# A gated mix of a long convolution and local attention: x transposed on the way in, and three groups of loads put elsewhere in their queue

## The chip, the cores and the metric

The kernel runs on one core of a Trainium2 chip. The core has a matrix engine (TensorE, PE in the profile; its weight loads are PEld), a vector engine (VectorE, DVE), a scalar engine (ScalarE, ACT), GpSimd (POOL) and a small engine that here only issues transfers (SyncE, SP). Sixteen DMA engines move data for all of them. Each engine runs its own instructions in order and waits on semaphores for the others. The metric is the device time of one execution in microseconds; the number of record is the median over the runs.

## The reference

S is 2048 positions, D is 640 channels, everything is bfloat16. Two branches are computed and mixed by a gate:

```python
x = A_q
g = sigmoid((x * gate_w).sum(-1, keepdims=True))
return g * a + (1 - g) * b

# a: shift convolution (4 taps) of k, times v, then a long causal convolution by FFT, times q
kv = k_shift * v
y  = irfft(rfft(kv padded to 2S) * rfft(ssm_k padded to 2S))[:S] + kv * ssm_D
a  = q * y

# b: attention of 32 heads of 20 channels; each position looks at 8 earlier
#    positions, two apart, itself included
q, k, v = split(x @ wqkv)
b = softmax(q k^T / sqrt(20)) v  @ wo
```

## The kernel before, in words

**A planner writes the order.** The kernel describes its work as generators (`loads`, `transposes`, `vproj`, `qkproj`, `fragger`, ...). Each yields requests: an engine, a cost in ns, the events it depends on, PSUM slots. A small list scheduler (`Plan`) picks at each step the request with the earliest start plus 120 ns times a priority from the table `PR`, and the instructions are emitted in that order. So the order on every engine, and on the SP queue, is settled when the kernel is built; an event in the plan that has no data behind it moves an instruction in the order but adds no wait on the chip. DMA issues on SP go round eight completion semaphores, so an issue waits until the eighth issue before it has landed.

**Attention first.** x is loaded in four chunks into `xS` with positions on partitions (even positions, then odd ones, since attention looks back in steps of two). TensorE transposes it in 128x128 blocks (L520), and the blocks are copied from PSUM into `xT` (channels on partitions, L277 and L279), which has gaps of seven zero columns ahead of each half. From `xT` come the values (`psv`, L540, in two halves of the channels) and the queries and keys (`pj`, L602). Queries and keys are copied out to `Gs` and `sH`, and POOL moves each head's 20 rows ("fragments", L638) to three rotating sets `qb` and `kb`. For eight groups of four heads: scores (`sc`, L668), exponential on ScalarE (L676), values (`O`, L702), and division on VectorE (L714, L716) into `oS`.

**Convolution beside it.** VectorE computes the four taps and the product with v in four blocks (L480 to L497); the product is written to DRAM (`kv_scr`) and read back in another layout. The filter `ssm_k` comes in two halves (`load_h`) over the place of the used k blocks; POOL adds `ssm_D` to its first sample (L802). The long convolution is a two-stage transform of 4096 points: stage 1 (L738) with `F1b`, stage 2 (L760) with the 2 MB matrix `G`, which takes the place of the staging `Gs`, first for the filter (`Hs`), then for kv (`X`). Complex products need a copy of the filter's spectrum with its two partition halves exchanged ("turned"): `swaps` makes it by DMA, group by group of channels, L835, and for the last group in two halves, L844, the second of which must wait for the multiplies of the first pass. `mults` (L858, L862) multiplies in two passes, groups 0 to 2 and groups 3 and 4, four blocks each. `inverse1` (L875) needs the blocks of its pass, `inverse2` (L950) needs all of `inverse1`, the matrix `T` (loaded over the last turned group once pass two is done) and q, which is loaded again as `qg` and scaled by the gate (L927).

**End.** Attention's output is transposed (L894), multiplied by `wo` (L988), scaled by 1 - g on the way out of PSUM (L995), moved to q's layout by POOL's DMAs (L1004), added (L1012) and stored (L975).

The order of the SP queue around the change, by its emission before:

```
x0 (two parts), Wv0, x1, x2, x3, Wqk ...
... kv stores 3 2, filter half 0, kv stores 1 0, G, filter half 1, kv back, wo
... swaps of groups 0 to 3, first half of group 4, 12 loads of q,
    second half of group 4, 4 loads of q, T, stores of the output
```

Of the kernel before, what the change touches and what calls it, by code (L numbers as in the profile page):

```python
# [144 lines left out]

PR = {'warm': -10.0, 'loads': 0.0, 'o_slot': -41.5, 'fragger': -30.7, 'score_gen': -0.4, 'pv_gen': -0.8, 'masks': 1.1, 'wcopy': 3.5, 'halo_gen': -13.7, 'conv': 17.2, 'transposes': 1.3, 'vproj': 2.4, 'gate': 2.4, 'qkproj': 3.1, 'h_diag': 16.3, 'h_stream': 1.9, 'open_p3': 26.5, 'swaps': -47.2, 'u_stream': 7.3, 'mults': -6.7, 'inverse1': 11.0, 'otrans': 10.8, 'outproj': 6.2, 'load_t': 18.2, 'load_q': 8.6, 'qscale': 0.8, 'adds': -3.0, 'inverse2': 25.0, 'vproj1': 4.5, 'vevict': -4.9, 'qevict': -6.0, 'opearly': 14.6, 'oplate': 22.1, 'vlean': 5.0, 'qlean': -169.0, 'slean': 204.0, 'ilean': 93.0, 'olean': 20.0, 'uh': 17.9}
HEAD = dict(A=130.0, D=60.0)
# [102 lines left out]
def kernel(  # L250
# [38 lines left out]
    ident = p0.tile([128, 128], BF, name="ident")  # L289
    xS = p0.tile([128, 16, D], BF, name="xS", tag="oS")  # L290
    Wv = p0.tile([128, NDT, D], BF, name="Wv", tag="wo")
# [39 lines left out]
    pL = Lx.enter_context(tc.tile_pool(name="pL", bufs=1, side="left", reuse_waits="tile"))  # L331
    xT = pL.tile([128, NDT, XW], BF, name="xT")
    Wqk = pL.tile([128, NDT, 2, D], BF, name="Wqk")
    pa = pL.tile([128, 4, D], BF, name="pa")
    pb = pL.tile([128, 4, D], BF, name="pb")
    wl = pL.tile([128, 4, D], BF, name="wl")

    W3 = B_wqkv.rearrange("(t p) (w n) -> p t w n", p=128, w=3)
# [3 lines left out]
    def ev(name):  # L342
        if name not in E:
            E[name] = Ev()
        return E[name]
# [10 lines left out]
    def loads():  # L356
# [4 lines left out]

        def load_x(c, k0=0, k1=4):
            yield from load(f"x{c}{k0}", xS[:, 4 * c + k0:4 * c + k1, :], xq4[:, c // 2, 4 * (c % 2) + k0:4 * (c % 2) + k1, :],
                            163840 * (k1 - k0), 1280)

        def nat(src, a):
            return raw(src, 4 * a * D, [[16 * D, 128], [1, 4 * D]])

        yield from load("ident", ident[:], ca["ident"].ap(), 32768, 256)
        yield from load_x(0, 0, 2)  # L370
        yield from load_x(0, 2, 4)
        yield from load("Wv0", Wv[:, :, 0:320], W3[:, :, 2, 0:320], 409600, 640)
        yield from load_x(1)
        yield from load_x(2)
        yield from load_x(3)
        def load_w(w, part, c0, c1):
# [59 lines left out]
    def pool_head():  # L436
        for c0, c1 in ((0, PRE), (HS, HS + PRE), (2 * HS, XW)):
# [12 lines left out]
        plan.at["G"] = 24000.0  # L450
# [61 lines left out]
    def transposes():  # L512
        for c in range(4):
            for k0, k1, d0, nd in ((0, 2, 0, 5), (2, 4, 0, 5)) if c == 0 else ((0, 4, 0, 4), (0, 4, 4, 1)):
                nk = k1 - k0
                g = yield Req("P", 56.0 * nk * nd, [ev(f"x{c}{k0}"), ev("ident")], take=1, ins=nk * nd)
                tr = psum(g, "trx", (128, 16 // nk, 128 * nk), BF)
                for dd in range(nd):
                    for k in range(nk):
                        nc.tensor.transpose(tr[:, dd, 128 * k:128 * k + 128], xS[:, 4 * c + k0 + k, 128 * (d0 + dd):128 * (d0 + dd) + 128], ident[:, :])  # L520
                w = 128 * nk * nd
                r = yield Req("AD", dict(A=190.0 + 0.834 * w, D=150.0 + 0.54 * w), [g.done], give=g.banks)
                o = ccol(4 * c) + 128 * k0
                copy(r.eng, xT[:, d0:d0 + nd, o:o + 128 * nk], tr[:, 0:nd, :])
                mark(f"xT{c}{k0 + d0}", r)
        mark("xS", r)

    def xdeps(c):
        return [ev(f"xT{c}{d}") for d in (0, 4 if c else 2)]

    def vproj():
        for half in range(2):
            c0 = 320 * half
            for b0 in range(0, NB, 2):
                nb = min(2, NB - b0)
                g = yield Req("P", 5 * nb * 136.0, xdeps(min(3, (b0 + nb - 1) // 4)) + [ev(f"Wv{half}")], take=1, pri=PR["vproj"] if half == 0 else PR["vproj1"], ins=5 * nb)
                ps = psum(g, "psv")
# [78 lines left out]
    def fragger():  # L616
# [10 lines left out]
        for t in range(NT):  # L627
            for f, w, h in sorted(todo[t]):
# [197 lines left out]
    def swaps():  # L826

        for g in range(NG):
# [10 lines left out]
            for hf in range(2):  # L839
# [5 lines left out]
                for k in range(2):  # L845
                    mark(f"hw{g}{2 * hf + k}", r)

    def mults():
# [54 lines left out]
    def load_q():  # L903
        yield Req("G", 1.0, [ev("us1")])
# [110 lines left out]
    def o_slot():  # L1015
        yield Req("G", 1.0, [ev("xS")])
        oS = p0.tile([128, NB, D], BF, name="oS", tag="oS")
        st["oS"] = oS
        x = ev("oSfree"); x.t = 0.0
# [62 lines left out]
```

## Time and profile before

| | |
|---|---|
| median of 8 runs | 241.11 us (240.37 to 242.01) |
| the profiled execution | 241.75 us |
| its span, first to last instruction | 240.0 us |
| mean granted TensorE clock in it | 0.906 |
| DMA | 42.57 MB, mean 177 GB/s |

The profile is of one execution. Its span is shorter than its time by what lies around the first and the last instruction. A timeline line has the start and the length in us, the engine, the line of the kernel, the operation with its output and input, how many it covers, and in brackets how long the engine had been idle before it and what released it. A table by stage has, for each stretch, its length, the busy time of PE, PEld, DVE, ACT and POOL (with counts), the granted clock, the busy share of the DMA engines and GB/s. TensorE's busy time is an upper view, since matmuls overlap.

### The profile page before, as it was taken

To read this page: it belongs to the slowest core of one execution; us is meant where nothing else is said; L and a number is where in the kernel's file an instruction comes from. 1 tells how busy PE (TensorE), PEld (TensorE's weight loads), DVE (VectorE), ACT (ScalarE), POOL (GpSimd) and SP (SyncE) were. 2 spreads that over 40 slices of the span, in tenths; PEclk is the share of its full clock that TensorE was granted. 3 is DMA by queue.
4 is the path that set the end of the run, shared out by engine and by line. 5 is a ranking of instruction groups with operands and counts; after the bars stand their busy time and mean duration, and the time that the engine had idled before them with its cause. 6 is when DMAs were issued, how large, how long until landed. Compare 5 with 4: busy or idle time off the path is not lost. (4 is left out here: it accounts for less than half of the span.)

```text
span 240.0 us, 8121 instructions
## 1 busy us (share of the span) xinstructions
PE 209.3 (87%) x3526; PEld 157.6 (66%) x3526; DVE 172.5 (72%) x214; ACT 183.7 (77%) x225; POOL 68.0 (28%) x137
## 2 busy tenths in 40 slices
PE   7999999999999999888866999989799959999800
PEld 3775645555555566565645788778689949989700
DVE  0567457988797797878784999898997095069760
ACT  4438588779899898889994998899999955943520
POOL 8803721396706053150000000000303030047520
PEclk9999999999999999955555899999999997999955
DMA  6997599767779822399999509995699916015872
GB/s 185 354 331 286 104 291 307 231 165 226 190 145 175 207 53 62 115 202 206 159 175 332 196 3 201 208 201 97 141 193 196 188 43 195 11 57 162 232 216 56
DMA packets 52579, 42.57 MB, mean 177 GB/s; under 512 B 27216, under 2 KB 47824, under 8 KB 52544
## 3 DMA queue, kind: packets, MB, share of 16 engines
q1 hardware_dynamic: 47664, 32.70, 56.4%
q0 software_dynamic: 4688, 9.03, 14.5%
q8 instruction: 27, 0.44, 0.8%
q10 hardware_dynamic: 192, 0.33, 0.5%
q14 instruction: 8, 0.07, 0.1%
HBM read 23.51 MB, written 5.25 MB: 120 GB/s over the span
## 5 line engine op out<-in xcount | busy, mean ns | idle before, releaser
L676 ACT ACTIVATE ET<-sc 128x726 bf16<-128x726 f32 (+1 forms) x80 | 64.9, 863 | 5.1 <-PE sc L668 4.7
L602 PE MATMUL pj<-xT,Wqk 128*128 128x363 bf16 (+3 forms) x250 | 48.4, 343 | 0.0
L1004 POOL DMA_DIRECT2D bl<-room x32 | 16.8, 529 | 82.3 <-ACT room L995 82.3
L602 PEld LDWEIGHTS <-Wqk 128*128 128x128 bf16 x250 | 22.9, 97 | 18.4
L279 DVE CAST Hs<-s 128x1024 bf16<-128x1024 f32 (+1 forms) x26 | 28.6, 1145 | 4.3 <-PE s L738 4.2
L277 ACT CAST X<-s 128x1024 bf16<-128x1024 f32 (+1 forms) x32 | 28.0, 987 | 0.2
L540 PE MATMUL psv<-Wv,xT 128*128 128x320 bf16 x170 | 24.9, 299 | 0.4 <-DMA Wv<-in_B_wqkv_dram 0.4
L875 PE MATMUL i<-M,Hs 128*128 128x128 bf16 x160 | 21.9, 235 | 3.2 <-DVE Hs L858 2.9
L988 PE MATMUL op<-wo,Hb 128*128 128x320 bf16 x160 | 23.9, 301 | 0.4 <-ACT X L277 0.2
L277 ACT CAST X<-i 128x1024 bf16<-128x1024 f32 x20 | 19.8, 1072 | 5.4 <-PE i L875 5.4
L875 PEld LDWEIGHTS <-Hs 128*128 128x128 bf16 x160 | 20.9, 151 | 3.3 <-DVE Hs L858 3.2
L875 PE MATMUL i<-M,X 128*128 128x128 bf16 x160 | 21.8, 234 | 0.5 <-DVE X L862 0.5
L760 PEld LDWEIGHTS <-Gs 64*128 64x128 bf16 x512 | 18.6, 95 | 5.4 <-issue 4.9
L988 PEld LDWEIGHTS <-Hb 128*128 128x128 bf16 x160 | 21.3, 145 | 1.1 <-issue 0.2
L668 PE MATMUL sc<-qb,kb 31*128 31x121 bf16 x544 | 18.8, 243 | 3.4 <-DVE oS L716 1.1
L875 PEld LDWEIGHTS <-X 128*128 128x128 bf16 x160 | 20.8, 151 | 0.8 <-DVE X L862 0.8
L995 ACT ACTIVATE room<-op,omg 128x640 bf16<-128x640 f32 x16 | 13.1, 820 | 10.3 <-PE op L988 10.3
L540 PEld LDWEIGHTS <-xT 128*128 128x128 bf16 x170 | 16.1, 98 | 6.9 <-issue 0.5
L638 POOL DMA_DIRECT2D qb<-Gs x21 | 11.5, 552 | 32.2 <-ACT Gs L277 20.5
L668 PEld LDWEIGHTS <-kb 31*128 31x128 bf16 x544 | 10.4, 102 | 14.3 <-issue 11.7
L277 ACT CAST Hs<-s 128x1024 bf16<-128x1024 f32 (+1 forms) x18 | 15.4, 909 | 3.6 <-PE s L738 2.2
L702 PEld LDWEIGHTS <-ET 128*128 128x128 bf16 x544 | 15.9, 100 | 3.4 <-issue 1.9
(77 smaller groups left out, 351.3 us busy)
## 6 DMA issues: line engine op xcount, KB each, us to landing
X<-Hs SPq DMA_DIRECT2D x16, 256.0 KB, 6.6
Hb<-in_A_k_dram SPq DMA_DIRECT2D x4, 640.0 KB, 10.3
kv<-in_A_v_dram SPq DMA_DIRECT2D x4, 640.0 KB, 12.7
kv_scr<-Hb SPq DMA_DIRECT2D x8, 320.0 KB, 4.2
Hb<-in_A_ssm_k_dram SPq DMA_DIRECT2D x16, 160.0 KB, 4.5
kv<-kv_scr SPq DMA_DIRECT2D x8, 320.0 KB, 5.4
bl<-room POOLq DMA_DIRECT2D x32, 80.0 KB, 3.2
qg<-in_A_q_dram SPq DMA_DIRECT2D x16, 160.0 KB, 7.2
```

Of the source, the lines that this page charges most:

```text
L277: nc.scalar.copy(dst, src)
L279: nc.vector.tensor_copy(dst, src)
L540: nc.tensor.matmul(ps[:, bb, 0:320], lhsT=xT[:, dt, BP * (b0 + bb):BP * (b0 + bb) + 128], rhs=Wv[:, dt, c0:c0 + 320], start=(dt == 0), sto ...
L602: nc.tensor.matmul(ps[:, i, 0:n], lhsT=Wqk[:, dt, w, 128 * ft:128 * ft + 128], rhs=rhs, start=(dt == 0), stop=(dt == NDT - 1))
L668: nc.tensor.matmul(scs[h4 // 2][:, h4 % 2, BP * bb:BP * bb + BP], lhsT=kb[r:r + DH + NF, 128 * b:128 * b + 128], rhs=qb[r:r + DH + NF, BP ...
L676: nc.scalar.activation(ETs[e][:, :, 0:nw], scs[hf][:, :, 0:nw], ACT.Exp, scale=SCALE)
L702: nc.tensor.matmul(O[:, o0:o0 + 21], lhsT=ET[:, hh, BP * bb:BP * bb + 128], rhs=VW[:, b, 4 * t + h4, :], start=True, stop=True, skip_group ...
L760: nc.tensor.matmul(ps[:, c, 0:64 * n * m].rearrange("p (a j l) -> p a j l", j=m, l=16)[:, :, jj, :], lhsT=G[rows, j, rr, :], rhs=raw(a, 20 ...
L875: nc.tensor.matmul(o, lhsT=piece(A[:, g:g + 1, :])[:, 0, c, :, :, 8 * oc + il].rearrange("p q j -> p (q j)"), rhs=M[:, k, :], start=(k == ...
L988: nc.tensor.matmul(op[:, k, 0:320], lhsT=raw(a, HS * (t % 2) + t // 2, [a.ap[0], [8, 128]]), rhs=wo[:, ft, 320 * k:320 * k + 320], start=( ...
L995: nc.scalar.activation(blt, op[:, :, 0:320], ACT.Copy, scale=omg[:, gcol(t):gcol(t) + 1])
L1004: nc.gpsimd.dma_start(bl[32 * gg:32 * gg + 32, t - 1:t + 1, :].rearrange("p t c -> p (t c)"), raw(row, 0, [[4 * pitch, 32], [1, 1280]]))
```

## The change

x is loaded straight into `xT` by five transposing DMAs of 256 to 512 positions (the first one ahead of `Wv0`), and the tile `xS` goes away. The odd half [...] first 9 and last 7 positions are loaded plainly into a corner of `wl`, transposed by five small TensorE transposes and copied in. The filter's second half is loaded ahead of `G` and planned behind POOL's last fragment; q's loads are planned behind the last swap. `xT` is wider (2080 columns instead of 2072, used through a shifted view). The priorities `PR` are those of a new search, so the order on all engines changes in places.

```diff
@@ tiles
-    xS = p0.tile([128, 16, D], BF, name="xS", tag="oS")
...
-    xT = pL.tile([128, NDT, XW], BF, name="xT")
+    xTt = pL.tile([128, NDT, 2080], BF, name="xT")
+    xT = xTt[:, :, 9:2080]
...
+    xs = wl[0:16, 0, :]
@@ loads
-        def load_x(c, k0=0, k1=4):
-            yield from load(f"x{c}{k0}", xS[:, 4 * c + k0:4 * c + k1, :], xq4[:, c // 2, 4 * (c % 2) + k0:4 * (c % 2) + k1, :],
-                            163840 * (k1 - k0), 1280)
+        def load_x(name, par, n0, n):
+
+            o = 16 + n0 if par == 0 else 9 + HS + PRE + n0
+            g = yield Req("S", 600.0, move=n * 5.4)
+            nc.sync.dma_start_transpose(xTt[:, :, o:o + n], raw(x2, (2 * n0 + par) * D, [[2 * D, n], [1, D]]))
+            mark(name, g)
...
+        yield from load_x("x0a", 0, 0, 256)
+        yield from load("Wv0", Wv[:, :, 0:320], W3[:, :, 2, 0:320], 409600, 640)
+        yield from load_x("x0", 0, 256, 256)
         yield from load("ident", ident[:], ca["ident"].ap(), 32768, 256)
-        yield from load_x(0, 0, 2)
-        yield from load_x(0, 2, 4)
-        yield from load("Wv0", Wv[:, :, 0:320], W3[:, :, 2, 0:320], 409600, 640)
-        yield from load_x(1)
-        yield from load_x(2)
-        yield from load_x(3)
+        yield from load("xs0", xs[0:9], raw(x2, D, [[2 * D, 9], [1, D]]), 11520, 1280)
+        yield from load("xs1", xs[9:16], raw(x2, (2 * 1017 + 1) * D, [[2 * D, 7], [1, D]]), 11520, 1280)
+        yield from load_x("x1", 0, 512, 512)
+        yield from load_x("x2", 1, 9, 512)
+        yield from load_x("x3", 1, 521, 496)
...
-            deps = [ev(f"st{a}{c}") for a in ((2, 3) if half == 0 else (0, 1)) for c in range(2)]
+            deps = [ev(f"st{a}{c}") for a in ((2, 3) if half == 0 else (0, 1)) for c in range(2)] + [ev("fraggo")] * half
...
         yield from store_kv(0)
+        yield from load_h(1)
         for jb in range(4):
             for d, h in zip(pieces(Gs[:, 2048 * jb:2048 * (jb + 1)]), pieces(cf["G"].ap()[:, 2048 * jb:2048 * (jb + 1)])):
                 yield from load(f"G{jb}", d, h, 262144, 1024, [ev("stg21"), ev("stg30"), ev("stg31")])
-            ev(f"G{jb}").t += 2000.0
-        yield from load_h(1)
@@ transposes
-        for c in range(4):
-            for k0, k1, d0, nd in ((0, 2, 0, 5), (2, 4, 0, 5)) if c == 0 else ((0, 4, 0, 4), (0, 4, 4, 1)):
...
-                        nc.tensor.transpose(tr[:, dd, 128 * k:128 * k + 128], xS[:, 4 * c + k0 + k, 128 * (d0 + dd):128 * (d0 + dd) + 128], ident[:, :])
...
+        g = yield Req("P", 250.0, [ev("xs1"), ev("ident")], take=1, ins=5)
+        tr = psum(g, "trx", (128, NDT, 16), BF)
+        for dd in range(NDT):
+            nc.tensor.transpose(tr[:, dd, :], xs[:, 128 * dd:128 * dd + 128], ident[0:16, 0:16])
+        r = yield Req("D", 200.0, [g.done])
+        nc.vector.tensor_copy(xT[:, :, HS + PRE:HS + PRE + 9], tr[:, :, 0:9])
+        r = yield Req("D", 200.0, give=g.banks)
+        nc.vector.tensor_copy(xT[:, :, HS + PRE + 1017:HS + PRE + 1024], tr[:, :, 9:16])
+        mark("xsm", r)
@@ fragger
+        x = ev("fraggo"); x.t = plan.at["G"]
@@ swaps
+        x = ev("swapped"); x.t = plan.at["S"]
@@ load_q
-                r = yield Req("S", 900.0, [ev("us1")], move=us(327680, 1280) * 1.4)
+                r = yield Req("S", 900.0, [ev("us1"), ev("swapped")], move=us(327680, 1280) * 1.4)
```

In the new order the SP queue reads: x (first 256 positions), Wv0, x (next 256), the identity, the two small loads, the rest of x, Wqk; later kv stores, filter half 1, G, kv back; later all swaps, all sixteen loads of q, T. The store of the gate's row to DRAM, which followed the loads of k and v, now stands after the first two of them.

More of the change, by code (lines that the diff above doesn't have):

```diff
@@ L143 @@
 LAT = {("P", "A"): 230.0, ("P", "D"): 230.0, ("A", "P"): 120.0, ("D", "P"): 120.0, ("A", "D"): 100.0, ("D", "A"): 100.0}
-PR = {'warm': -10.0, 'loads': 0.0, 'o_slot': -41.5, 'fragger': -30.7, 'score_gen': -0.4, 'pv_gen': -0.8, 'masks': 1.1, 'wcopy': 3.5, 'halo_gen': -13.7, 'conv': 17.2, 'transposes': 1.3, 'vproj': 2.4, 'gate': 2.4, 'qkproj': 3.1, 'h_diag': 16.3, 'h_stream': 1.9, 'open_p3': 26.5, 'swaps': -47.2, 'u_stream': 7.3, 'mults': -6.7, 'inverse1': 11.0, 'otrans': 10.8, 'outproj': 6.2, 'load_t': 18.2, 'load_q': 8.6, 'qscale': 0.8, 'adds': -3.0, 'inverse2': 25.0, 'vproj1': 4.5, 'vevict': -4.9, 'qevict': -6.0, 'opearly': 14.6, 'oplate': 22.1, 'vlean': 5.0, 'qlean': -169.0, 'slean': 204.0, 'ilean': 93.0, 'olean': 20.0, 'uh': 17.9}
+PR = {'warm': -10.0, 'loads': 0.0, 'o_slot': -49.2, 'fragger': -47.0, 'score_gen': -0.9, 'pv_gen': 2.2, 'masks': 8.5, 'wcopy': 1.8, 'halo_gen': -26.2, 'conv': 14.4, 'transposes': -7.1, 'vproj': 1.0, 'gate': 2.0, 'qkproj': 3.0, 'h_diag': 0.3, 'h_stream': 3.5, 'open_p3': 42.1, 'swaps': -52.4, 'u_stream': 9.0, 'mults': -8.3, 'inverse1': 9.4, 'otrans': 8.0, 'outproj': 8.1, 'load_t': 18.8, 'load_q': 0.3, 'qscale': 9.8, 'adds': 6.2, 'inverse2': 25.2, 'vproj1': 3.6, 'vevict': 1.8, 'qevict': -6.4, 'opearly': 15.4, 'oplate': 21.3, 'vlean': 56.0, 'qlean': -211.0, 'slean': 340.0, 'ilean': 156.0, 'olean': -158.0, 'uh': -3.6}
 HEAD = dict(A=130.0, D=60.0)
@@ L436, in pool_head @@
     def pool_head():
-        for c0, c1 in ((0, PRE), (HS, HS + PRE), (2 * HS, XW)):
+        for c0, c1 in ((0, PRE), (HS, HS + PRE), (2 * HS, 2071)):
             nc.gpsimd.memset(xT[:, :, c0:c1], 0.0)
@@ L512, in transposes @@
     def transposes():
-        for c in range(4):
-            for k0, k1, d0, nd in ((0, 2, 0, 5), (2, 4, 0, 5)) if c == 0 else ((0, 4, 0, 4), (0, 4, 4, 1)):
[L515 to L519, printed above, removed]
-                        nc.tensor.transpose(tr[:, dd, 128 * k:128 * k + 128], xS[:, 4 * c + k0 + k, 128 * (d0 + dd):128 * (d0 + dd) + 128], ident[:, :])
[L521 to L526, printed above, removed]
+        g = yield Req("P", 250.0, [ev("xs1"), ev("ident")], take=1, ins=5)
[7 more added lines that the diff above has]
+        mark("xsm", r)
     def xdeps(c):
-        return [ev(f"xT{c}{d}") for d in (0, 4 if c else 2)]
+        return [ev(f"x{c}")] + ([ev("xsm")] if c >= 2 else [])
     def vproj():
@@ L535, in vproj @@
                 nb = min(2, NB - b0)
-                g = yield Req("P", 5 * nb * 136.0, xdeps(min(3, (b0 + nb - 1) // 4)) + [ev(f"Wv{half}")], take=1, pri=PR["vproj"] if half == 0 else PR["vproj1"], ins=5 * nb)
+                g = yield Req("P", 5 * nb * 136.0, (xdeps(min(3, (b0 + nb - 1) // 4)) if b0 else [ev("x0a")]) + [ev(f"Wv{half}")], take=1, pri=PR["vproj"] if half == 0 else PR["vproj1"], ins=5 * nb)
                 ps = psum(g, "psv")
@@ L903, in load_q @@
     def load_q():
-        yield Req("G", 1.0, [ev("us1")])
+        yield Req("G", 1.0, [ev("us1"), ev("swapped")])
         qg = p0.tile([128, 16, D], BF, name="qg", tag="kv")
@@ L1015, in o_slot @@
     def o_slot():
-        yield Req("G", 1.0, [ev("xS")])
+        yield Req("G", 1.0)
         oS = p0.tile([128, NB, D], BF, name="oS", tag="oS")
```

## The prediction, on record before the changed kernel ran

> **What bounds the kernel now.** I read the page for the engines' shares, then a table of busy time by stage, then the chain of waits, and last the timeline at each place where that table shows slack. One engine doesn't bound the kernel: the bound changes by stage.
>
> ```profile
> PE 209.3 (87%) x3526; PEld 157.6 (66%) x3526; DVE 172.5 (72%) x214; ACT 183.7 (77%) x225; POOL 68.0 (28%) x137
> ...
> 0.00:25.00 25.00, 23.38 (x176) 15.18 (x177) 12.72 (x14) 13.12 (x14) 13.01 (x30) 1.00 0.87 281
> 25.00:100.00 75.00, 74.19 (x980) 43.99 (x978) 59.18 (x65) 63.64 (x87) 32.61 (x64) 1.00 0.68 172
> 100.00:128.00 28.00, 20.38 (x515) 15.55 (x511) 20.51 (x30) 25.35 (x33) 4.55 (x9) 0.55 0.98 196
> 128.00:179.00 51.00, 46.61 (x897) 40.65 (x898) 47.14 (x50) 46.82 (x54) 2.14 (x4) 0.95 0.77 173
> 179.00:210.00 31.00, 27.44 (x373) 26.85 (x372) 15.24 (x30) 24.89 (x28) 4.17 (x8) 0.94 0.63 128
> ```
>
> The columns of the lower lines are stretch, length, PE, PEld, DVE, ACT, POOL busy, granted clock, DMA share, GB/s. To 100 us TensorE is never free (97.57 of 100). From 100 to 128 it is ScalarE (25.35 of 28) with DMA full (0.98). From 128 to 179 VectorE and ScalarE are both over 90%. From 179 to 210 nobody is full: something there waits. Two timeline places tell what the waits are:
>
> ```profile
> 124.93 0.49 PE L668 MATMUL sc<-qb,kb 31*128 31x121 bf16 x12 [0.40 <-DVE oS L716]
> 127.29 0.56 POOL L802 TENSOR_TENSOR Hb<-Hb,Dz 128x80 bf16<-128x80 bf16 x1 [22.20 <-DMA Hb<-in_A_ssm_k_dram]
> 127.91 1.21 PE L738 MATMUL s<-F1b,Hb 64*128 64x128 bf16 x16 [2.49 <-POOL Hb L802]
> 129.16 1.01 ACT L277 CAST Hs<-s 128x1024 bf16<-128x1024 f32 x1 [2.20 <-PE s L738]
> ```
>
> The filter's second half lands at 127.3. TensorE waits 2.49 us for it, and ScalarE then waits 2.20.
>
> ```profile
> 171.17 8.01 SPq L911 DMA_DIRECT2D qg<-in_A_q_dram  x12
> 179.73 2.65 SPq L844 DMA_DIRECT2D X<-Hs  x2
> 182.63 2.78 SPq L911 DMA_DIRECT2D qg<-in_A_q_dram  x4
> ...
> 191.51 1.23 DVE L858 TENSOR_TENSOR Hs<-X,Hs 128x2048 bf16<-128x2048 bf16 x1 [6.75 <-ACT X L277]
> 193.45 2.45 DVE L927 TENSOR_SCALAR qg<-qg,g_nat 128x640 bf16<-128x640 bf16 x8
> 198.35 0.69 DVE L862 TENSOR_TENSOR X<-X 128x1024 bf16<-128x1024 bf16 x1
> ...
> 197.69 0.28 PE L875 MATMUL i<-M,Hs 128*128 128x128 bf16 x1 [2.94 <-DVE Hs L858]
> 198.49 0.33 PE L875 MATMUL i<-M,X 128*128 128x128 bf16 x1 [0.52 <-DVE X L862]
> ```
>
> VectorE stops at 184.75 for 6.75 us. The named releaser, an eviction, had long been done: L858 overwrites the part of Hs that the last swap (L844) reads, and that swap was issued behind twelve q loads. Then eight q scalings (2.45 us) stand in VectorE's order ahead of the last multiplies, which release the inverse's groups 3 and 4. ScalarE starves in turn.
>
> **Part 1: x by transposing loads.** It removes 80 PE transposes and 8 evictions (six on VectorE, two on ScalarE). The first 20 transposes (4.85 to 7.14) ran while Wv was in flight (psv starts at 7.50), so they cost nothing. The others took 2.17, 0.40, 1.06 and 0.39 us: 4.0 us on an engine that doesn't stop before 30 us. Five 16-column transposes are added, at the 0.06 us pitch of the old ones: 0.3 us; their wait for the 16 odd rows sits behind ten psv matmuls. The evictions lay in VectorE's early slack (12.72 of 25): nothing.
>
> The loads themselves are new here. The nearest row is the plain x load: 346 GB/s between 10 and 20 us, so 2.62 MB take 7.6 us. The Trainium skill (DMA: Bandwidth & Descriptors, section Latency and other measured facts) gives 261 GB/s for a transposing DMA of a non-contiguous source: by it an estimate of 10.0 us. No trace here has one; being slower, the rule speaks against the change, and I take it. Then the q/k weights, next in the same queue, land 2.4 us later: pj, which began at 14.9, can begin at 17.3. Does TensorE wait for that? The new order puts 70 psv matmuls ahead of pj. From about 6 us (Wv0 is now behind 256 rows of x, not 512) 70 at 0.144 us (20 in 2.88) are 10.1, plus 0.3 for the small transposes and 1.3 for a first ten at the cold pace (the first 20 transposes took 0.115 us each, later ones 0.06): 17.7 us. The cover is only 0.4 us; by the plain rate it is 2.8, and the sum is the same. Every microsecond beyond the cover costs one.
>
> From there: 50 pj matmuls at 0.178 (40 in 7.12) 8.9, 10 psv 1.5, gate 1.3, 5 psv 0.8: 30.2 us. Before, that same work, plus two score groups of some 1.3 us with their waits, ended at 34.4, so 33.1 without them. Part 1 gives **2.9 us**. SP's issue of a plain x load took 0.51 us at the median; five even at 2 us each add 7.5 us, and 4.7 us of issues before the q/k weights become 12, still ahead of 17. The two loads of odd rows (11 KB each) and the identity move next to nothing; the identity's issue took 0.37 us. The gate's scratch store now precedes the v and k loads on SP and holds them to about 30 us, where the first v was issued at 28.55; conv uses that v at 40, so some 4 us of cover remain. If it went, VectorE's conv would move by the excess. On POOL the halo's memset (1.69 us) and load now precede two fragments of the second head group, and the memset waits for the first conv block: about 41 us, so those fragments go out at 43.3, where they went at 46.3: 0. If conv slips past 44, they slip with it, and the scores that need them.
>
> **Part 2: filter half before matrix G.** Now eight G loads (2.1 MB), then eight filter loads whose issues take 17.42 us, because an issue waits for the eighth before it. In the new order the filter follows the kv stores at once. Its first half took 68.44 to about 81.9 (last issue 77.4, plus the 4.5 us median): 13.4 us beside fragments. With the stores landed at about 100 (98.9 for conv, 4.2 to land, less part 1) it lands at 113.4, long before its use. The 2.49 and 2.20 us waits go: **2.3 us**. What is late next? G: 9.5 us at 220 GB/s, to 123, against its first reader at 130.2 less 5.2 = 125; only a quarter is needed then. kv: 2.6 MB at the 390 GB/s seen from 128 to 134, to 130, against 140. If G's cover of 2 us is gone, the gain is lost one for one. The last fragments share the DMA with the filter instead of G; their POOL order is kept, and the diagonal add stays after them.
>
> **Part 3: q behind the last swap.** The swap, issued by 182.4, is no longer behind 2 MB of q; with the swaps' median landing, 6.6 us from 181, it lands near 188, and the last two multiply blocks (2.5 us each) end at 193 instead of 199. The inverse's first three groups keep TensorE and ScalarE until about 194, so nothing waits. What bounds the stretch is then ScalarE's eviction of all twenty inverse tiles (about 1.0 us each). It was idle 5.76 us between 179 and its last tile at 209.03 (30.03 less 24.27 busy). I count 4.8, leaving 1 us for unevenness. Two tiles of outproj move to before the inverse, where ScalarE is full as well: no change in its sum. Next to be late: q, 2.6 MB at 195 GB/s behind the swap, lands at 198.5, and T (1.05 MB at 250 GB/s), behind q on SP, at 202.7; needed at 204.2. Cover 1.5 us. Part 3: **4.8 us**.
>
> **New search.** The other orders move too. All six evictions of the transposed attention output go to VectorE (1.12 us, where ScalarE took 1.68), and kv casts go to ScalarE in exchange. I bound this by -1 and +1.5 us (both engines are over 90% there, so a bad order shows) and take 0: rows per engine hardly change. The last 30 us have the same order as before.
>
> Sum: 2.9 + 2.3 + 4.8 = 10.0. The profiled execution took 241.75 us (span 240.0 and 1.75 around it); 231.75 after, and its run lay 0.64 above the median 241.11, so **231.1**.
>
> **Rivals.** (a) Slow transposes, the one that ends slower. The filter loads, in 128-byte runs, moved 1.31 MB in 13.4 us: 98 GB/s. If transposed blocks move like those, x takes 26.7 us, the q/k weights land at 34, and TensorE stands 16 us: 241.1 - 10.0 + 16.3 = 247.4. It decides from x taking about 20 us (under 130 GB/s), where the stall equals the three gains. For: a transpose must scatter small pieces, and nothing in the trace shows one. Against: the rate given by the page. 0.12. (b) The gains don't add: ScalarE has 11 us idle of 75 between 25 and 100, so its exponentials may not start sooner just because TensorE is 2.9 us ahead, or T or G comes late by 2 us. Half of part 1 and 2.5 us of the rest lost: 235. 0.25. (c) The new order puts a wait that cancels all, such as VectorE held in order behind an eviction (it waited 5.7 us for psv at 27): 241 to 243. 0.05. (d) The rearrangement gives no more than it says and all three hold: 227.5 to 234. 0.58.
>
> **Numbers.** (d) is likeliest: 231.1. Faster takes (d), (b) and a little of (c): 0.84. A measurement here can't tell less than 0.3% (0.7 us); 0.02 lie within it, between (b) and (a). Slower 0.14: (a) and most of (c). The range, 227.5 to 239, holds (d) and (b) and leaves out most of (a) and (c).
>
> **What would show it.** Right: psv without a pause from 6 us and pj beginning by 18; the diagonal add near 112 and no idle TensorE before the last s1 pair; VectorE's gap before the third pass-1 multiply under 4 us; no q scaling between multiplies; twenty inverse evictions back to back. Wrong: TensorE idle for x or Wqk before 30 us (part 1), for G after 120 (part 2), for T before L950 (part 3).

## The result and the profile after

The changed kernel took **235.59 us** (median of 11 runs) against 241.03 us for the kernel before (32 runs): a ratio of 0.9762, 95% interval 0.9731 to 0.9793. It is faster by 5.4 us, where 10.0 were forecast; the forecast was 231.1 us with a range of 227.5 to 239. Its profiled execution took 234.66 us, with a span of 232.9 us and a mean granted clock of 0.925. Ratios leave out executions in a slower state (of the changed kernel those of 239.68 and 610.7 us), and the profiled execution of e8 below is one of these, so the table has no places for it.

First the busy times again: the line of the page, and the table by stage with the columns of before.

```profile
PE 203.2 (87%) x3451; PEld 150.5 (65%) x3451; DVE 173.1 (74%) x216; ACT 175.1 (75%) x217; POOL 68.4 (29%) x137
```

```profile
0.00:25.00 25.00, 20.06 (x112) 11.09 (x113) 7.76 (x10) 9.56 (x12) 10.02 (x26) 1.00 0.94 228
25.00:100.00 75.00, 72.24 (x935) 41.88 (x933) 61.67 (x67) 60.64 (x81) 36.07 (x68) 1.00 0.71 192
100.00:128.00 28.00, 22.59 (x563) 17.28 (x562) 21.68 (x32) 26.52 (x35) 4.54 (x9) 0.60 0.87 224
128.00:179.00 51.00, 47.23 (x886) 41.35 (x886) 48.77 (x52) 43.94 (x54) 4.22 (x8) 0.95 0.62 143
179.00:210.00 31.00, 30.88 (x600) 29.90 (x597) 19.72 (x37) 27.14 (x32) 5.60 (x11) 1.00 0.75 162
```

TensorE has 6.1 us less to do (203.2 after 209.3), most of it from the transposes. But it was busy for 97.57 of the first 100 us before, and is now for 92.30. The work that was taken away there left idle time behind. In the last row it is the other way round: 30.88 of 31 us busy, where it was 27.44. Slack has gone from the late part, and has come up at the start.

**Part 2** shows nearly as forecast, in the timeline of all engines:

```profile
102.28 11.56 SPq L360 DMA_DIRECT2D Hb<-in_A_ssm_k_dram  x8
116.53 0.57 POOL L804 TENSOR_TENSOR Hb<-Hb,Dz 128x80 bf16<-128x80 bf16 x1 [9.93 <-DMA Gs<-cf_G]
126.80 1.22 PE L740 MATMUL s<-F1b,Hb 64*128 64x128 bf16 x16 [0.15 <-ACT ET L678]
128.07 1.02 ACT L277 CAST Hs<-s 128x1024 bf16<-128x1024 f32 x1
```

The diagonal add stands at 116.5, where it was at 127.3 (near 112 was forecast). TensorE's wait ahead of the last stage-1 products is 0.15 us instead of 2.49, and ScalarE's 2.20 us are gone.

**Part 3** too. This is the timeline between 180 and 202 us:

```profile
180.25 14.19 SPq L914 DMA_DIRECT2D qg<-in_A_q_dram  x16
...
184.43 0.68 DVE L865 TENSOR_TENSOR X<-X 128x1024 bf16<-128x1024 bf16 x1
185.10 16.85 ACT L277 CAST X<-i 128x1024 bf16<-128x1024 f32 x18
186.21 1.23 DVE L861 TENSOR_TENSOR Hs<-X,Hs 128x2048 bf16<-128x2048 bf16 x1 [1.09 <-DMA X<-Hs]
...
190.68 0.68 DVE L865 TENSOR_TENSOR X<-X 128x1024 bf16<-128x1024 bf16 x1
193.35 0.39 DVE L930 TENSOR_SCALAR qg<-qg,g_nat 128x640 bf16<-128x640 bf16 x1 [1.99 <-issue]
195.05 1.32 SPq L923 DMA_DIRECT2D X<-cf_T  x2
```

VectorE's gap ahead of the third multiply block is 1.09 us instead of 6.75, and its releaser is now named rightly: the swap, landed by 186.2. The multiplies end at 191.4 instead of 199.0, all q scalings come after them, and ScalarE evicts eighteen inverse tiles in one piece (twenty were forecast).

**Part 1** does not show as forecast. From the timeline of the first 32 us:

```profile
0.76 1.39 SPq L367 DMA_TRANSPOSE xT<-in_A_q_dram  x1
...
6.57 8.90 SPq L367 DMA_TRANSPOSE xT<-in_A_q_dram  x3
7.20 2.83 PE L541 MATMUL psv<-Wv,xT 128*128 128x320 bf16 x10 [2.41 <-DMA Wv<-in_B_wqkv_dram]
13.04 1.53 PE L541 MATMUL psv<-Wv,xT 128*128 128x320 bf16 x10 [1.33 <-DMA xT<-in_A_q_dram]
14.62 5.61 PE L541 MATMUL psv<-Wv,xT 128*128 128x320 bf16 x40
15.51 1.16 SPq L360 DMA_DIRECT2D Wqk<-in_B_wqkv_dram  x2
18.31 1.89 SPq L360 DMA_DIRECT2D Hb<-in_A_k_dram  x2
20.06 9.17 PE L603 MATMUL pj<-xT,Wqk 128*128 128x484 bf16 x50
31.69 1.49 DVE L485 TENSOR_TENSOR pa<-Hb,wl 128x2560 bf16<-128x2560 bf16 x1 [7.26 <-DMA Hb<-in_A_k_dram]
```

psv begins at 7.2 us, not at 6, and waits once more for x. pj follows the last psv without a wait, at 20.06 (17.7 was forecast; 14.9 before). The transposing loads keep SP busy issuing until 15.5 us, so that the q/k weights, and behind them the k rows, are issued late. The weights still land in time for pj; the k rows don't for the convolution, which begins at 31.69, where it began at 24.34.

How fast x came is read from slices of 2.5 us (columns as in the table by stage), after first, then before:

```profile
5.00:7.50 2.50, 0.30 (x2) 0.21 (x3) 0.00 (x0) 1.67 (x1) 2.23 (x3) 1.00 1.17 241
7.50:10.00 2.50, 2.50 (x11) 1.15 (x10) 0.00 (x0) 0.00 (x0) 2.50 (x6) 1.00 0.95 184
10.00:12.50 2.50, 1.72 (x16) 1.05 (x15) 2.14 (x4) 0.70 (x1) 0.99 (x2) 1.00 1.11 219
```

```profile
5.00:7.50 2.50, 2.14 (x20) 1.98 (x19) 1.15 (x2) 1.74 (x1) 2.04 (x3) 1.00 1.04 327
7.50:10.00 2.50, 2.50 (x19) 1.81 (x19) 1.70 (x2) 0.69 (x1) 2.50 (x5) 1.00 1.06 377
10.00:12.50 2.50, 2.50 (x42) 2.31 (x41) 1.19 (x2) 1.28 (x2) 1.19 (x3) 1.00 1.14 330
```

The DMA engines are full in both. They move 184 to 241 GB/s where they moved 327 to 377; over all six slices from 2.5 to 17.5 us the mean is 217 after 333.

### The profile page after: what moved, and what is told of

Its sections match the earlier page's. It is cut to its first block, busy times and chain, and to the rows that moved or that the text cites. A ratio compares the mean times of both kernels' runs of the same rounds, so it can differ in the third digit from the quotient of the medians.

```text
span 232.9 us, 7970 instructions
## 1 busy us (share of the span) xinstructions
PE 203.2 (87%) x3451; PEld 150.5 (65%) x3451; DVE 173.1 (74%) x216; ACT 175.1 (75%) x217; POOL 68.4 (29%) x137
## 2 busy tenths in 40 slices
DMA packets 60803, 42.57 MB, mean 183 GB/s; under 512 B 37472, under 2 KB 56048, under 8 KB 60768
## 4 chain that ended last, share of the span: by engine, by line
PE 40%; DVE 20%; ACT 12%; DMA 12%; SPq 8%; issue 4%; ACTq 1%; DVEq 0%
PE pj L603 10%; PE i L878 9%; PE op L991 7%; ACT ET L678 6%; DMA Hb<-in_A_k_dram 5%; SPq L367 5%; DVE Hs L279 4%; PE psv L541 4%; ACT X L277 3%; PE O L704 3%; DMA kv<-kv_scr 3%; DVE X L279 3%; PE s L762 3%; SPq L360 3%; DVE Hb L279 2%
## 5 line engine op out<-in xcount | busy, mean ns | idle before, releaser
L678 ACT ACTIVATE ET<-sc 128x726 bf16<-128x726 f32 (+1 forms) x80 | 64.1, 864 | 5.2 <-PE sc L670 4.8
L277 ACT CAST X<-s 128x1024 bf16<-128x1024 f32 (+1 forms) x33 | 29.5, 963 | 4.9 <-PE s L740 3.9
L541 PE MATMUL psv<-Wv,xT 128*128 128x320 bf16 x170 | 26.9, 309 | 4.3 <-DMA Wv<-in_B_wqkv_dram 2.4
L878 PE MATMUL i<-M,Hs 128*128 128x128 bf16 x160 | 20.5, 227 | 0.1
L277 ACT CAST Gs<-pj 128x968 bf16<-128x968 f32 (+5 forms) x18 | 13.5, 750 | 9.5 <-PE pj L603 6.6
L878 PE MATMUL i<-M,X 128*128 128x128 bf16 x160 | 20.4, 226 | 0.0
L878 PEld LDWEIGHTS <-Hs 128*128 128x128 bf16 x160 | 20.2, 149 | 0.3
L670 PE MATMUL sc<-qb,kb 31*128 31x121 bf16 x544 | 18.0, 240 | 2.6 <-ACT ET L678 1.3
L639 POOL DMA_DIRECT2D qb<-Gs x21 | 10.6, 508 | 29.3 <-ACT Gs L277 17.2
L277 ACT CAST X<-i 128x1024 bf16<-128x1024 f32 x20 | 19.0, 1165 | 0.0
L670 PEld LDWEIGHTS <-kb 31*128 31x128 bf16 x544 | 10.1, 101 | 12.5 <-issue 9.7
```

What stands on the lines that cost most here:

```text
L277: nc.scalar.copy(dst, src)
L541: nc.tensor.matmul(ps[:, bb, 0:320], lhsT=xT[:, dt, BP * (b0 + bb):BP * (b0 + bb) + 128], rhs=Wv[:, dt, c0:c0 + 320], start=(dt == 0), sto ...
L670: nc.tensor.matmul(scs[h4 // 2][:, h4 % 2, BP * bb:BP * bb + BP], lhsT=kb[r:r + DH + NF, 128 * b:128 * b + 128], rhs=qb[r:r + DH + NF, BP ...
L678: nc.scalar.activation(ETs[e][:, :, 0:nw], scs[hf][:, :, 0:nw], ACT.Exp, scale=SCALE)
L878: nc.tensor.matmul(o, lhsT=piece(A[:, g:g + 1, :])[:, 0, c, :, :, 8 * oc + il].rearrange("p q j -> p (q j)"), rhs=M[:, k, :], start=(k == ...
```

## The experiments

Times are medians; each ratio is against the kernel before, run beside it on the same chip. The other columns are places in one profiled execution, in us, which took up to 1.7 us more or less than the median: the end of the last scores (sc), the start of stage 2 of the convolution's transform (`s<-Hs,Gs`), the stretch from the first multiply to the end of the inverse's evictions, and the tail from there to the last addition.

| kernel | time | ratio, 95% interval | last scores | stage 2 | multiplies to inverse | tail |
|---|---|---|---|---|---|---|
| before | 241.03 | 1 | 125.42 | 130.22 | 46.3 | 24.7 |
| after | 235.59 | 0.9762 [0.9731, 0.9793] | 126.65 | 129.14 | 39.6 | 25.1 |
| e1, part 3 alone | 238.42 | 0.9896 [0.9842, 0.9951] | 124.99 | 129.53 | 40.1 | 26.7 |
| e2, part 2 alone | 239.34 | 0.9919 [0.9877, 0.9960] | 126.28 | 128.77 | 46.0 | 24.5 |
| e3, parts 2 and 3, old order | 235.28 | 0.9768 [0.9724, 0.9811] | 125.30 | 127.79 | 40.1 | 26.7 |
| e4, parts 2 and 3, new order | 238.51 | 0.9896 [0.9848, 0.9945] | 129.19 | 131.69 | 39.6 | 25.4 |
| e5, all parts, old order | 238.70 | 0.9891 [0.9831, 0.9950] | 129.82 | 131.90 | 39.8 | 26.6 |
| e6, transposing loads on ACT | 252.22 | 1.0456 [1.0395, 1.0516] | 145.00 | 147.50 | 39.6 | 24.6 |
| e7, half of x transposed by loads | 234.70 | 0.9739 [0.9683, 0.9794] | 124.57 | 129.03 | 39.5 | 24.8 |
| e8, q scalings last, alone | 237.84 | 0.9822 [0.9750, 0.9894] | | | | |
| e9, e3 with the new late order | 236.17 | 0.9803 [0.9739, 0.9867] | 125.56 | 129.70 | 39.6 | 24.7 |
| e10, e7 with the old front | 237.72 | 0.9867 [0.9802, 0.9933] | 128.77 | 130.79 | 39.6 | 25.3 |
| e11, after with the old front | 238.25 | 0.9887 [0.9825, 0.9949] | 129.95 | 132.04 | 39.6 | 25.2 |
| e12, after with less convolution | 234.83 | 0.9798 [0.9750, 0.9846] | 126.38 | 128.87 | 39.6 | 25.2 |

An "order" here is a set of priorities, the line `PR`. The old one is that of before, the new one that of after. A "front" is the part of it that governs the work up to the first diagonal products, "late" the rest.

**e1: part 3 alone.** In the kernel before:

```diff
@@ swaps
+        x = ev("swapped"); x.t = plan.at["S"]
@@ load_q, both requests
-        [ev("us1")]
+        [ev("us1"), ev("swapped")]
```

> The kernel before with part 3 alone: q's loads planned behind the last swap. The order changes only from the first multiply on; the sixteen q scalings now stand behind the last multiply. Theory (what the prediction said): the swap no longer waits behind 2 MB of q, VectorE's 6.75 us gap before the third pass-two block shrinks to 1 to 3 us, the inverse's evictions run without a pause on ScalarE: 4.5 to 6 us faster than before, ratio near 0.979. Rival (the gain after came from the new search, not from this): under 1 us, ratio over 0.996.

Measured: 2.5 us (1.2 to 3.8), less than expected. The stretch from the first multiply to the inverse's end is shorter by 6.2 us, more than the 4.8 forecast. But the tail behind it is 2.0 us longer.

**e2: part 2 alone.**

```diff
@@ fragger
+        x = ev("fraggo"); x.t = plan.at["G"]
@@ loads: load_h(1) ahead of G, its deps with ev("fraggo"); then
-            ev(f"G{jb}").t += 2000.0
```

> The kernel before with part 2 alone: the filter's second half loaded ahead of G. Theory: the 2.49 us that TensorE waited at 125 and ScalarE's 2.20 go, G is still in time: 2 to 2.5 us faster, ratio near 0.990. Rival: the q stall later hides it, or G and kv are now late by as much: within 0.5 us of before.

Measured: 1.9 us (1.0 to 3.0), as forecast within the interval.

**e3: both, with the old order and plain loads of x.** That is the change without part 1 and without the new search.

> The kernel before with parts 2 and 3, old priorities, x still by plain loads and 80 PE transposes. If the two moves add and part 1 brought nothing or cost something (reading of the trace after: the last scores come 1.2 us later than before): 6.5 to 8 us faster than before, 233 to 234.5, at or below the changed kernel's 235.6. If part 1 is worth the 2.9 us of the prediction: the changed kernel without it, about 238.5.

Measured: 235.28 us, the time of the changed kernel: 5.7 us gained, where 6.5 to 8 were expected. The two moves alone bring everything; part 1 and the new search together bring nothing that these runs can tell.

**e4 and e5: part 1 against the order.** e4 has the new order with plain loads, e5 all of the change with the old order. With e3 and after they fill a square of four.

> The same as the run before, with the priorities of the changed kernel: the changed kernel without part 1. It tells part 1 at equal priorities. Theory (part 1 costs about 1 us, from the slow transposing loads): 233.5 to 235. Rival (part 1 gains 2.9 us): 238 to 239. The priorities were searched with part 1 in place, so some loss through an order that doesn't fit is possible; then this run is above the previous one.

> The changed kernel with the old priorities, so the two moves with plain loads at old priorities (235.3) plus part 1. Theory 1 (the prediction's part 1: 4 us of transposes gone from a full TensorE): 2.4 to 3 us below, 232.3 to 233. Theory 2 (the slow x transfers delay pj and the k loads by as much as the transposes free): 235 to 236. Theory 3 (each set of priorities fits its own front, as the run with the new ones and plain loads suggested with 238.5): 237 to 239.

With the old order the transposing loads cost 3.0 us (0.9768 to 0.9891); with the new order they gain 3.2 (0.9896 to 0.9762). In both rows the intervals lie apart. "What part 1 is worth" has no one answer: each order does better with the loads of its own kernel, and the wrong pairing costs 3 us either way. The granted clock has a part in these 3 us; that comes after e11.

**e6: the transposing loads issued by ScalarE,** so that SP's queue stays free for the others.

```diff
-            nc.sync.dma_start_transpose(xTt[:, :, o:o + n], ...)
+            nc.scalar.dma_start_transpose(xTt[:, :, o:o + n], ...)
```

> The changed kernel with its five transposing loads issued by ScalarE instead of SP; all else keeps its order. If the issue of a transposing load (1.4 us for 256 rows, 2.97 for 512 in the trace after) is what holds the loads behind it on SP, then Wqk, pa and k are issued by 7 us instead of 20, conv starts near 27 instead of 31.7, and the run is 0.5 to 2 us faster than the changed kernel. If the DMA engines themselves are full with x (share 0.95 to 1.18 in the trace after from 2.5 to 17.5 us at about 220 GB/s), x lands later by what the others take first, conv gains 2 us at most, pj comes later, and the time is the same within 1 us or worse.

Measured: 11.0 us slower than before (4.56%). The timeline of the first 40 us:

```profile
0.74 27.26 ACTq L367 DMA_TRANSPOSE xT<-in_A_q_dram  x5
31.98 6.74 PE L541 MATMUL psv<-Wv,xT 128*128 128x320 bf16 x30 [17.07 <-ACT VW L277]
38.56 6.70 PE L603 MATMUL pj<-xT,Wqk 128*128 128x484 bf16 x35
```

The five issues that took 11.8 us on SP (1.39, 1.48 and 8.90) took 27.26 us here, with plain loads running beside them. So an issue has no fixed price. I read it as the issuing engine being held while the loads ahead drain; no run shows that apart. ScalarE could evict nothing for 28 us, and TensorE stood 17.07 us for it. From 20 to 37 us its granted clock was then 0.5, so that the thirty psv above took 6.74 us, where thirty took 4.25 in e5. The k rows did come 3.6 us earlier (the convolution began at 28.05), which is the order of loads that was wanted, at the wrong price.

**e7: only the odd half of x by transposing loads,** the even half loaded plainly and transposed on TensorE as before; new order.

```diff
-        yield from load_x("x0a", 0, 0, 256)
...
-        yield from load_x("x1", 0, 512, 512)
+        yield from load_p(0, 0, 2)
+        yield from load_p(0, 2, 4)
...
+        yield from load_p(1)
```

> The changed kernel with only the odd half of x by transposing loads; the even half is loaded plainly and transposed by 40 TensorE instructions, new priorities. Psv starts as before and pj near 17, conv near 28; TensorE carries 2 us more than the changed kernel. If the late front is what costs part 1 its gain: 234 to 235.5. If TensorE's work to 100 us decides: 236.5 to 237.

Measured: 234.70 us. pj begins at 17.88, between 14.9 and 20.06 (here it does wait for the q/k weights, 1.19 us), and the convolution at 28.77. The time is the changed kernel's, within the intervals. The profiled execution is the slowest of the six: 236.43 us at a mean clock of 0.904, where the others have 0.923 to 0.925.

**e8: the q scalings behind the last multiply, alone.** SP's order stays that of before.

```diff
-            r = yield Req("D", 230.0, [ev(f"qg{t // 8}"), ev("gate")])
+            r = yield Req("D", 230.0, [ev(f"qg{t // 8}"), ev("gate"), ev("m13")])
```

> The kernel before with one dependency more: q's scalings stand behind the last multiply on VectorE; the SP queue keeps its order, so the last swap still waits behind twelve q loads. It parts the two halves of the q stall. Theory: the swap's 6.75 us gap stays, only the 2.45 us of eight scalings go: 1 to 2.4 us faster, ratio 0.990 to 0.996. Rival (the gap was the wait for q, not for the swap): as the first run of this study, ratio near 0.99 with the gap gone.

Measured: 4.3 us (2.6 to 6.0), above what was expected and not less than e1, which moves the loads too. The one profiled execution still has the swap's gap ahead of the third multiply block:

```profile
194.19 1.23 DVE L858 TENSOR_TENSOR Hs<-X,Hs 128x2048 bf16<-128x2048 bf16 x1 [5.95 <-DMA X<-Hs]
```

Its stretch from the first multiply to the inverse's end is 41.8 us, where it was 46.3. So the gain seems to lie there, with the gap still in place. From one execution of 240.78 us that is an indication only, and how part 3 divides between the swap and the scalings stays open.

**e9: e3 with the new late order.** Does the longer tail of e1, e3 and e5 cost anything?

```diff
-PR = {... 'h_diag': 16.3, 'h_stream': 1.9, ... 'uh': 17.9}
+PR = {... 'h_diag': 0.3, 'h_stream': 3.5, ... 'uh': -3.6}
```

> x loaded plainly and transposed on TensorE as before; the filter half and q moved as in the change; the old search's priorities for everything up to the first diagonal products, the new search's for everything later. This separates the two halves of the new search. Theory: with the old priorities the plan leaves one outproj tile and one more unit of the second inverse behind the last inverse eviction, and the stretch from there to the last addition takes 26.6 to 26.7 us in the three runs with those priorities and part 3, against 25.1 to 25.4 in the two runs with the new ones. So the later priorities alone give 1.4 us more than the run of both moves in the old order: 233.9 us, and the stretch 25.2. Rival A: the tile only moves to before the inverse, where ScalarE is full, so that the gain is paid there: 235.3, with the stretch from the first multiply to the last inverse eviction 1.4 us longer than its 40.1. Rival B: the loss of 3.2 us that the new priorities brought with plain loads lies in the later part and not in the front: 238.5.

In the timeline of TensorE the old late order (e3) has five groups of outproj, of 20 matmuls each, behind the last eviction of the inverse (200.05 us), and a short unit of the second inverse, which waits, at the very end:

```profile
216.56 2.94 PE L989 MATMUL op<-wo,Hb 128*128 128x320 bf16 x20
220.08 0.36 PE L951 MATMUL i<-X 32*32 32x160 bf16 x32 [0.58 <-DVE qg L966]
```

The new late order (e9) has four such groups behind that eviction (202.91 us), and one longer last unit without a wait. Its stage 2 waits for an eviction that doesn't hold up e3:

```profile
129.70 0.82 PE L760 MATMUL s<-Hs,Gs 64*128 64x192 bf16 x8 [1.11 <-ACT Hs L277]
...
216.94 2.94 PE L989 MATMUL op<-wo,Hb 128*128 128x320 bf16 x20
219.81 1.37 PE L951 MATMUL i<-X 32*32 32x160 bf16 x128
```

The tail is 24.7 us, 2.0 shorter, as the theory said. The time is not: 236.17 us. The first multiply comes 3.45 us later than in e3 (163.36 after 159.91), 1.9 of it already at the start of stage 2. Rival A has the direction right, but in these two profiles the price is paid ahead of the multiplies, not behind them. Two microseconds that the table shows so plainly at the end of the kernel brought no gain that can be measured.

**e10 and e11: the old front with the new late order,** for e7 and for the changed kernel.

> The changed kernel with the even half of x loaded plainly and transposed on TensorE, and only the odd half by transposing loads, now with the old search's priorities up to the first diagonal products and the new ones later. The same half with all new priorities took 234.70. Theory (each set of priorities fits the loads that it was searched for): the half lies between the two, so the old front costs it about as much as it gains, within 1.5 us of 234.7. Rival A (the old front is the better one wherever k lands by 25 us, since it starts the convolution at 24 us): 233.2 or less. Rival B (the old front costs 3 us as soon as any of x comes by a transposing load): 237.7.

> The changed kernel whole, all of x by transposing loads, with the old search's priorities up to the first diagonal products and the new ones later. With all old priorities it took 238.70. Theory: of the 3.1 us by which that is over the changed kernel, 1.5 lie in the stretch after the last inverse eviction (26.6 against 25.1 us), and the rest in the front, whose last scores end 3.2 us later: 237.2. Rival A: the front's order is worth nothing and all comes from the later part: 235.6. Rival B: all comes from the front: 238.7.

e11 takes 238.25 us, as with all old priorities: the whole loss of e5 is in the front (rival B). e10 takes 237.72, 3.1 us over e7 in the ratio, so the theory for it fell and its rival B stands: the old front costs 3 us as soon as half of x comes by a transposing load. With plain loads the front costs 2.2 us the other way (e9 to e4), though there the intervals overlap. Among the kernels with parts 2 and 3, the time follows the start of stage 2: at 130.8 to 132.0 us in the mismatched four (e4, e5, e10, e11), at 127.8 to 129.7 in the five whose front suits their loads (after, e3, e7, e9, e12).

**The clock beside these runs.** The order is not all that differs. In every profile but e6's, where it comes later, TensorE's granted clock falls to half between 99 and 108 us and comes back between 131 and 138. Two rows (columns as in the table by stage), the changed kernel and then e11:

```profile
98.00:104.00 6.00, 4.73 (x112) 3.25 (x111) 4.44 (x7) 5.32 (x8) 1.39 (x3) 1.00 0.62 163
128.00:134.00 6.00, 5.87 (x117) 5.60 (x117) 5.43 (x8) 4.96 (x7) 0.00 (x0) 0.59 0.83 302
```

```profile
98.00:104.00 6.00, 4.54 (x134) 3.44 (x131) 4.17 (x7) 5.90 (x8) 3.08 (x7) 0.81 0.75 195
128.00:134.00 6.00, 5.39 (x110) 4.31 (x108) 5.24 (x9) 4.34 (x7) 0.00 (x0) 0.50 1.00 368
```

Eight matmuls of stage 2 take 0.82 us at half clock and 0.51 at full (the changed kernel, at 129.14 and 137.11 us). Ahead of the tail, the time at half clock is 27.3 us in the changed kernel, e3 and e12, 30.7 in e1, e2 and e9, 34.1 in the kernel before, e4, e5, e7 and e11, and 37.6 in e10.

It shows in the times too. In each of the seven kernels that have executions on both sides of a mean clock of 0.915, those above it are faster, by 1.1 to 2.0 us. Of the 22 executions counted for the changed kernel, e3 and e7, 18 lie above; of the 23 of the mismatched four, one does; of the 43 of the kernel before that stand beside e1 to e12, twelve do, so part of each gain in the table may be the clock's. Below 0.915 alone, the mismatched four average 237.8 to 238.8 us, and the changed kernel, e7, e9 and e12 236.2 to 236.6. So about 2 of the 3 us remain at a like clock, and the rest goes with the clock. (This is rough: the kernel before, run beside them, has medians from 240.3 to 241.9.) The two profiles of e7 (236.43 us, 0.904) and e10 (236.23, 0.902) show no loss at all. Whether an order that doesn't fit brings the longer half clock, and by what, no run here tells.

**e12: is it VectorE?** This asks what took back the gain of part 1 in the changed kernel. The convolution begins 7.4 us later in the changed kernel, and its eight instructions per block then run in one piece. In the changed kernel, for the first two blocks:

```diff
+            w = D // 2 if a >= 2 else D
...
-                nc.vector.tensor_tensor(pa[:], pa[:], pb[:], ALU.add)
+                nc.vector.tensor_tensor(pa[:, :, 0:w], pa[:, :, 0:w], pb[:, :, 0:w], ALU.add)
```

> The changed kernel, every engine's order as it is, with the first two of the four convolution blocks computed for half of the channels only (320 of 640): the other half of their output is left out. That takes 0.75 us from each of sixteen VectorE instructions that run between 31.7 and some 58 us, 12 us in all, and starts the two blocks' stores earlier. It asks whether the convolution, begun 7.4 us late behind the k loads, is what took back the time that part 1 saved on TensorE. In the changed kernel TensorE is idle for 2.76 us of the stretch from 25 to 100 us (0.89 with plain loads and the old order), and 1.6 us of its waits there name VectorE's attention output. Theory (VectorE, full from 40 to 80 us, holds back the attention's outputs and so TensorE): the waits for it before 60 us go, TensorE's idle time from 25 to 100 falls to about 1.5 us, the last scores end about 1.3 us earlier, near 125.3, and the kernel takes 234.3. Rival A (the fragments' transfers, with DMA busy 0.95 between 40 and 60, hold TensorE back): idle stays over 2.4 us, the waits turn into waits for qb and kb, and the time stays at 235.6. Rival B (more than VectorE's order: all of part 1's 2.9 us comes free): 232.7.

TensorE's waits between 25 and 100 us (engine, its instruction, the releaser; total, times, longest), first in the changed kernel, then in e12:

```profile
PE pj L603 <- DVE oS L718: 1.6, 2, 1.0
PE psv L541 <- ACT ET L678: 0.4, 1, 0.4
PE O L704 <- ACT ET L678: 0.4, 1, 0.4
```

```profile
PE O L708 <- ACT ET L682: 0.9, 2, 0.5
PE pj L607 <- DVE oS L722: 0.4, 1, 0.4
PE psv L545 <- ACT ET L682: 0.4, 1, 0.4
```

And the same stretch by busy time: e3, then the changed kernel's row shown above against e12.

```profile
25.00:100.00 75.00, 74.11 (x982) 43.94 (x980) 58.83 (x65) 63.59 (x87) 32.61 (x64) 1.00 0.67 173
```

```profile
25.00:100.00 75.00, 72.83 (x945) 42.31 (x944) 51.91 (x69) 61.21 (x81) 36.11 (x68) 1.00 0.77 197
```

The wait of 1.0 us for VectorE went, and VectorE has 9.8 us less to do. TensorE's idle time fell only from 2.76 to 2.17 us, and the last scores end 0.27 us earlier: part of the gain came back as longer waits for exponentials, and pj had begun 0.33 us later. The time is within the intervals of the changed kernel's. The waits did not turn into waits for qb and kb either, so rival A fell as well. Of the lost time, these two blocks on VectorE account for about 0.6 us. What carries the rest was not isolated.

## Why the prediction was right, and where it was off

The direction was right, and parts 2 and 3 did what was forecast of them. The size was off by 4.5 us. So (d), held likeliest at 0.58, is out, and the time is that of rival (b), "the gains don't add: 235", given 0.25. Its split is not: (b) lost half of part 1 and 2.5 us of the rest, and the runs lose all of part 1 and 1.4 us of the rest. "Faster" came out right by parts 2 and 3, which bring it without part 1; on part 1 the argument was wrong, and the range held because it left room for (b).

**Part 2 (forecast 2.3).** Right. Stage 2 begins 2.4 us sooner in e3 (130.22 to 127.79) and 1.45 in e2, which gains 1.9 us. The forecast of what is late next held too: neither G nor kv shows as a wait of TensorE's.

**Part 3 (forecast 4.8).** The mechanism was right: the swap landed by 186.2 (188 forecast), the multiplies ended at 191.4 (193), the second inverse began at 203.55 (T needed at 204.2), and ScalarE became the bound. The stretch itself gained 6.2 us in e1 and 6.7 in the changed kernel. As forecast, q and T arrived without a new wait on TensorE. Yet parts 2 and 3 together brought 5.7 us (4.6 to 6.6), not the 7.1 of the sum. In e3's profile the tail is 2.0 us longer. That could be the missing term, but e9, whose tail is short again, took no less (236.17), with five of its six executions at a lower clock than any of e3's. The 1.4 us stay open.

**Part 1 (forecast 2.9).** This is the step that failed: the term "from about 6 us, 70 psv matmuls, so 17.7". Wv landed for 7.2, the third ten psv waited 1.33 us for x, and pj began at 20.06: 2.4 of the 2.9 us were gone there. The forecast had taken for x the 261 GB/s that the Trainium skill gives ("DMA: Bandwidth & Descriptors", section Latency and other measured facts), so 10.0 us. The trace shows a mean of 217 GB/s from 2.5 to 17.5 us for everything that was moving, at a full DMA share; x was still being issued at 15.5. The last of its loads was issued at 12.5 and, by the median landing of 5.8 us, landed at about 18. So x alone, 2.6 MB, took some 17.5 us: an estimate of 150 GB/s. A second part of the same step: SP's five issues were bounded at "2 us each", ending at 12 us; they took 11.8 us together and ended at 15.5. The cover of 0.4 us, beyond which every microsecond was to cost one, was not what failed: it was meant for the q/k weights, and pj did not wait for them. Their arrival had been dated by pj's start in the kernel before (14.9), where no wait for them shows either. The time was lost ahead of pj.

The remaining loss was not in the forecast's sum; only rival (b) hinted at it. From 25 to 100 us TensorE stood idle for 2.76 us where it had been 0.81, so another 1.95 us went. 2.9 - 2.4 - 1.95 is -1.45: and the first diagonal product starts at 100.56 us, 1.4 later than in e3 (99.16). The forecast assumed that an engine which is full stays full when work is taken from it. What made the idle time is shown for about 0.6 us (e12); the cause of the rest stays open.

**The new search (forecast 0, bounds -1 and +1.5).** Wrong in kind. The order is not a small term beside part 1 but its other half: worth about +3 us with the transposing loads, and -3 us without them, the clock's share included. The bounds should have been as wide as the loads' own term, which the order was fitted to.

**The covers.** The gate's store was forecast to hold the v rows to 30 us; they were issued at 35.08, and the product that uses them came at 42.71. The halo's memset came at 44.3, 41 having been forecast, so the fragments behind it went out at 46.4 and not at 43.3, as the text had said they would if the convolution slipped past 44 (its first block ended at 44.20). POOL then stood 3.60 us for a DMA (the halo's load, by the profile) and put out the next fragments at 53.5; e3 has them out from 49.2. No wait of TensorE names a fragment, and no run tried it. The rival of slow transposes (a) was nearer than its 0.12: x alone came at about 150 GB/s, between the 130 from which it would have decided and the 346 of plain loads.

No version that was run beats the changed kernel by more than its interval: e3, e7 and e12 (which leaves work out) lie within 0.9 us of it.

## What to carry to other kernels

Work taken from a full engine is a gain only if the engine's other work can start earlier by as much. Ask for the replaced work's inputs first: here the transposes cost TensorE 4 us, but the transfers that replaced them had the loads behind them in the queue issued 5 to 11 us later (k at 18.31 after 12.85, the q/k weights at 15.51 after 4.72). When a kernel's order is searched anew with each edit, price edit and order together, or test all four pairings: with the order that fits the other kernel, part 1 costs 3 us, and with its own it gains 3. Read the granted clock beside each time before a few microseconds are given to an order. And a stretch at the end that is plainly shorter in the table proves nothing until the time moves with it.

## What the runs showed of the hardware

Transposing loads of x (1280-byte rows, every other row) kept the DMA engines full at 184 to 255 GB/s in the slices from 2.5 to 17.5 us, against 288 to 377 for the same stretch with plain loads. Issuing them holds the issuing engine: 1.4 to 1.5 us for 256 positions and 2.9 to 3.0 for about 512 on SP, but 27.26 us for all five on ScalarE with plain loads running beside. That was not expected; a plain load of x took 0.51 us to issue. The page counts 37472 packets under 512 bytes, after 27216: by an estimate the 2.6 MB went in packets of some 250 bytes.

TensorE's time at half clock came in like steps. It adds up to 27.3, 30.7 or 34.1 us around 100 to 137 us, to 3.4 where a profile has one short dip besides, and to 17.1 in e6 from 20 to 37 us. That is 8, 9, 10, 1 and 5 times 3.41 us.
